# A new order of work for a decode block with its gradients: priorities, load gates and eviction bias

## The chip, the cores and the metric

The kernel runs on one core of a Trainium2 chip. Time is the device time in microseconds (us) of one execution, smaller is better. Times are given as the median of several runs; the profile is of one further execution, whose own time stands beside its span.

## The reference

The kernel computes one decode step of a transformer block, its output and the gradients of all inputs that have one. With `x` of shape 2 x 1 x 576 (two batch elements, one token each):

```python
xn = layernorm(x)
out = x + A(xn, k_cache, v_cache, wq, wo) + B(xn, w_gate, w_up, w_down)
# A: grouped-query attention, 32 query heads, 16 K/V heads, 4096 cached positions, head size 128
q = xn @ wq;  p = softmax(q @ k.T * 128 ** -0.5);  A = (p @ v) @ wo
# B: bilinear gated MLP, hidden width 4608
B = ((xn @ w_gate) * (xn @ w_up)) @ w_down
outputs = out, gradients of x, k_cache, v_cache, wq, wo, w_gate, w_up, w_down
```

All tensors are bf16. The K and V caches are 2 x 16 x 4096 x 128 (32 tiles of 1 MB each), and their gradients have the same size. The gradients are outer products of short vectors, so the kernel reads 92.48 MB, writes 92.48 MB, and does little arithmetic for each byte.

## The kernel before, in words

**Tiling.** The attention is cut into 16 steps (8 groups of two K/V heads, two batch elements); a step has two K tiles and two V tiles, each 128 x 4096 (1 MB). The MLP is cut into nine slices of 512 hidden columns, loaded in pairs. Sixteen SBUF buffers of 1 MB, called `big`, hold everything large: loaded K and V tiles, their transposed copies, gate and up weights, and the staging of results before they are stored. Six `ww` buffers hold wq, wo and w_down pieces.

**What a step does.** `turn` transposes a loaded tile on VectorE (DVE) in two halves (L418, 128x1024 f32). `score` multiplies it with the queries on TensorE (PE, L1205: 32 small matmuls per head). `softmax` and `dscore` are chains of small operations that hop between PE, DVE and ScalarE (ACT). `contract` (L1378) multiplies the probabilities with V, or the score gradients with K. `build_BD` makes a block-diagonal matrix on GpSimd (POOL, L1193). `head_outer` makes 1 MB of a cache gradient: PE writes outer products into one of three double PSUM banks `ps_o` (L1226), ACT or DVE casts them to bf16 in a `big` buffer (an eviction: L422 on ACT, L424 on DVE), and after four of these SP stores the buffer (`put`, L644). Gradients of the weights go the same way, by `rows_outer` (L675, 576 columns), `wide_outer` (L712) and `tails` (L756). In this layout out_2 is the gradient of K, out_3 that of V, out_4 of wq, out_5 of wo, out_6 and out_7 of gate and up, out_8 of w_down.

**Queues.** Every large load and store is issued by SP, one after the other (loads: L1087 for K and V, L1103 and L1107 for wq, L1112 for wo, L1126 and L1129 for gate and up, L1135 for w_down). An issue waits for the engines that fill or free its buffer, and for the landing of the transfer eight places before, since there are eight semaphores in turn. While SP waits, nothing behind it is issued. PE, ACT, DVE and POOL likewise run their instructions strictly in the program's order.

**What sets the order.** The kernel is written as some twenty generators (`turn`, `fronts`, `attend`, `dscores`, `load_kv` and so on) that yield their steps with an estimated cost: `PE(...)`, `DVE(0.34)`, `EV(1024)`, `DMA(...)`, `ACQ(...)` for a buffer. While the program is built, the class `Order` runs a small planner over them. It takes the step that can start first; of the steps that can start on the same engine no later than `SLACK[engine]` after it, it takes the one with the lowest priority number (`min` over the pair of priority and start), and the instructions are written down in that order. The priorities are the lists `PRI`: one number per step and kind of work, such as `out1` for the gradient of V. For POOL and SP the slack is 1e9, so there the priority alone decides among those that are known. `EV(cols)` is an eviction that may go to ACT or DVE: the planner takes the engine on which start, cost and bias are lowest, and DVE's bias is `cols / 1024 * BIAS`. `AT` holds load gates: a weight load may not be issued before the K or V load with that number (negative: no gate). Waits between engines are put in by the framework from the buffers that are read and written, so every order computes the same. On the chip nothing of the planner is left but the order.

Of the kernel before, what the change touches and what calls it, by code (L numbers as in the profile page):

```python
# [63 lines left out]
class Order:  # L64
# [88 lines left out]
    def run(self):  # L153
        while self.streams:
# [8 lines left out]
            if e is not None:  # L163
                t, _, s, e = min((c for c in cand if c[3] == e and c[0] <= t + SLACK[e]), key=lambda c: (c[1], c[0]))
            r = s.req
# [55 lines left out]
def EV(cols):  # L221
    return ("any", [("ACT", 0.16 + cols * 0.00083, 0.0), ("DVE", 0.145 + cols * 0.00104, cols / 1024 * BIAS)])

# [25 lines left out]
def DMA(engine, cost, nbytes, row=8192):  # L249
# [4 lines left out]
NBIG, NGU, NWW, NBD = 16, 1, 6, 3  # L254
CAP = {"kv": 7, "X": 15, "st": 4, "G": 2}
PRI = {
    "turn0": [7860.2, 2407.0, 17157.6, 2956.1, 16734.6, 2141.3, 12530.3, 5699.3, 6758.9, -15793.6, 4952.3,
        17816.5, -4355.6, 3251.1, -9409.0, 4354.9],
    "turn1": [-2637.0, 1283.6, 2414.9, -1225.0, -688.7, 9788.2, -4100.9, -1253.1, -13338.4, -4832.0, 7420.0,
        -4070.9, 3909.7, 3439.1, 24860.7, -8046.8],  # L260
    "W0": [5450.2, -3369.6, -7183.8, -9911.8, -15919.4, -4137.9, -34387.0, -4019.0, 12808.9, -13268.0, 2164.8,
        858.2, 9204.1, -21915.1, 27410.8, 5714.0],
    "W1": [-17967.7, -22162.9, -7000.7, 5860.0, -24123.9, -16750.0, -30695.7, -2322.8, 5885.0, -3621.0,
        -11899.3, -25222.7, 3484.3, 17013.0, 9916.4, -50953.1],
    "BD0": [25740.3, 53517.1, -7884.7, -22398.1, 2616.3, 11674.1, 17259.1, 25394.6, 12932.1, -24698.9, 82.6,
        -21163.1, -19953.8, 2102.0, 984.1, 27628.2],
    "BD1": [4904.3, 19218.9, 29867.0, 8059.0, 13597.2, -18879.4, 4713.9, 9772.5, 5835.6, -5651.5, 17495.2,
        -17656.1, 4419.6, -9395.9, -9786.8, -9239.0],
    "att": [-16176.1, -16637.1, -12810.8, -4457.5, 5838.0, -2018.2, -8215.2, -6231.2, -139.6, -20917.1,
        -13722.1, -15572.7, -14151.6, -16625.5, -17042.9, -18171.9],  # L270
    "dsc": [-9216.4, -7162.0, 2808.5, -17222.3, -6700.5, -8396.7, -1687.0, -19475.0, 11785.3, -22804.1,
        -13738.0, -25105.3, -15681.5, -29505.6, -519.1, -10067.7],
    "conv": [-73.6, -802.0, 808.6, 9911.0, -26988.3, -160.1, -15612.0, 2673.7, 20749.7, 20926.3, -10685.8,
        -20284.9, -8067.0, -18305.9, 1302.8, -5957.9],
    "con": [-3577.6, 11238.1, -10064.9, -5905.6, -14352.4, -9473.6, -2022.2, -31439.8, -4882.4, 8558.6, 647.3,
        -9042.3, -19399.9, -1065.6, -2476.7, 5001.6],
    "out0": [14046.8, 7812.4, 18755.6, 1578.1, 18723.0, 2045.3, -76.0, 4635.4, -4249.5, 66463.6, 1241.8,
        1393.3, 26893.0, 2322.7, -5773.2, 8123.2],
    "out1": [5636.0, 11913.1, 6780.7, 20338.1, 9883.3, -10850.1, 4408.6, 5776.7, 23687.8, 8619.3, 4031.8,
        17526.5, 33972.4, 22842.4, 6234.3, -887.1],  # L280
    "load": [3193.5, -640.3, 301.4, -16753.0, -8208.1, 1940.7, 9048.5, 16627.4, 5590.0, 7449.3, 8037.6,
        -5473.6, -4620.7, -10313.2, 936.0, -17873.6],
    "front": [11759.7, 4097.5, -19331.9, 3980.4, -367.3, 2898.4, -5242.4, -2790.9],
    "back": [-6458.1, -50.3, 4435.4, -11360.7, -12548.4, -12384.9, 955.9, -216.8],
    "mlp": [163.8, -787.4, -543.1, -7011.3, 1620.2, 3974.5, -1165.0, -2471.6, 1570.8],
    "mload": [-21609.9, -16477.7, -1378.7, -18105.2, 21631.6],
    "wload": [-1915.1, -8158.3, -15308.5, -12116.0, -16845.1, -3320.8, 11983.3, 9881.2, -10244.7, -12615.0,
        -8866.9, -18849.5, -7415.5, -20806.8, -24590.0, 27553.0],
    "wout": [-3012.7],
    "store": [2385.5],  # L290
    "fin": [-34927.4],
    "const": [23913.5],
}
AT = {
    "wq": [-17, 6, 5, 24, 30, -16, 50, -5],
    "wo": [-16, -13, -12, -7, 36, -20, -6, 52],
    "mlp": [2, 15, -12, 39, 82],
}
LATENCY, DRY, RATE = 0.5, 0.9, 1.009
LM, LAG, DRIFT = 0.67, 2.2, 0.009  # L300
CLK = 1.65
BIAS = 0.231829490117948
SLACK = {"PE": 0.0, "ACT": 0.11263292874939297, "DVE": 0.4671146883182233, "POOL": 1e9, "SP": 1e9}


def pr(name, i=0):
# [1227 lines left out]
```

## Time and profile before

| | |
|---|---|
| time, median of 3 runs | 474.47 us (472.94 to 476.24) |
| the profiled execution: its own time | 473.33 us |
| its span, first to last instruction | 471.3 us |
| mean granted TensorE clock | 0.718 of full |
| bytes moved by the DMA queue of SP | 184.96 MB, 395 GB/s over the span with the rest |
| instructions | 15,474 |

The page gives the busy time of each engine, and the span in 40 slices of 11.8 us: for each engine a digit for the tenths of the slice in which it was busy, for the DMA engines the share of time with packets, and the GB/s that they moved. An engine that waits in its own order for another shows idle time; the list of waits names whom it waited for. For SP, which only issues transfers, the list of waits says which engine's work the next transfer in its line was waiting for.

### The profile page before, as it was taken

To read this page: it belongs to the slowest core of one execution; us is meant where nothing else is said; L and a number is where in the kernel's file an instruction comes from. 1 tells how busy PE (TensorE), PEld (TensorE's weight loads), DVE (VectorE), ACT (ScalarE), POOL (GpSimd) and SP (SyncE) were. 2 spreads that over 40 slices of the span, in tenths; PEclk is the share of its full clock that TensorE was granted. 3 is DMA by queue.
4 is the path that set the end of the run, shared out by engine and by line. 5 is a ranking of instruction groups with operands and counts; after the bars stand their busy time and mean duration, and the time that the engine had idled before them with its cause. 6 is when DMAs were issued, how large, how long until landed. Compare 5 with 4: busy or idle time off the path is not lost. (4 is left out here: it accounts for less than half of the span.)

```text
span 471.3 us, 15474 instructions
## 1 busy us (share of the span) xinstructions
PE 368.2 (78%) x6636; PEld 214.5 (46%) x6636; DVE 372.2 (79%) x710; ACT 332.7 (71%) x502; POOL 147.2 (31%) x176
## 2 busy tenths in 40 slices
PE   0588688788787879795786779689699788988891
PEld 0455453454554344464353444464344544544461
DVE  9688787989857878878689748978867988888771
ACT  2158668678974967473798638877678788879881
POOL 3350242673330311300632354000744717034100
PEclk9987785879756677677866657956656677666785
DMA  8999999999999999999999999999999989999993
GB/s 309 407 407 415 392 388 378 357 417 411 423 420 419 396 419 422 428 411 417 414 418 386 385 418 421 414 397 360 412 412 377 424 302 424 423 406 396 425 406 127
DMA packets 40053, 185.96 MB, mean 395 GB/s; under 512 B 3496, under 2 KB 11184, under 8 KB 23600
## 3 DMA queue, kind: packets, MB, share of 16 engines
q1 hardware_dynamic: 39976, 184.96, 98.0%
q8 instruction: 52, 0.85, 0.7%
q14 instruction: 17, 0.14, 0.1%
q10 hardware_dynamic: 8, 0.00, 0.0%
HBM read 92.48 MB, written 92.48 MB: 392 GB/s over the span
## 5 line engine op out<-in xcount | busy, mean ns | idle before, releaser
L422 ACT CAST big<-ps_o 128x1024 bf16<-128x1024 f32 (+3 forms) x317 | 277.8, 951 | 41.2 <-PE ps_o L1226 20.4
L418 DVE STREAM_TRANSPOSE big<-big 128x1024 f32<-128x1024 f32 x146 | 176.1, 1223 | 9.0 <-DMA out_dram<-big 2.4
L1193 POOL TENSOR_TENSOR BD<-vr,mask 128x2048 bf16<-128x2048 bf16 x32 | 115.3, 3604 | 204.6 <-ACT vr L422 126.3
L424 DVE CAST big<-ps_o 128x1024 bf16<-128x1024 f32 (+3 forms) x73 | 80.3, 1100 | 20.3 <-PE ps_o L1226 7.5
L1205 PE MATMUL ps_m<-big,W 128*32 128x128 bf16 x2048 | 58.0, 275 | 7.7 <-issue 2.5
L1205 PEld LDWEIGHTS <-W 128*32 128x32 bf16 x2048 | 45.9, 121 | 26.4 <-issue 23.7
L1226 PE MATMUL ps_o<-BD,dd 32*128 32x512 bf16 x256 | 44.9, 460 | 13.9 <-ACT big L422 10.7
L1226 PE MATMUL ps_o<-BD,pp 32*128 32x512 bf16 x256 | 46.0, 490 | 11.1 <-ACT big L422 6.7
L1170 POOL COPY W<-rep 32x16 bf16<-32x16 bf16 x128 | 24.8, 194 | 49.3 <-DVE rep L951 40.2
L418 DVE STREAM_TRANSPOSE big<-ww 128x1152 f32<-128x1152 f32 (+1 forms) x25 | 33.0, 1318 | 1.2 <-PE ps_m L1378 0.7
L1378 PE MATMUL ps_m<-big,pp 128*32 128x512 bf16 x256 | 29.0, 543 | 2.3 <-DVE pp L418 1.5
L1378 PE MATMUL ps_m<-big,dd 128*32 128x512 bf16 x256 | 26.0, 496 | 1.3 <-DVE dd L418 0.8
L1226 PEld LDWEIGHTS <-dd 32*128 32x128 bf16 x256 | 11.6, 96 | 33.8 <-issue 27.9
L1226 PEld LDWEIGHTS <-pp 32*128 32x128 bf16 x256 | 10.6, 96 | 30.6 <-issue 26.6
L422 ACT CAST osb<-ps_m 128x512 bf16<-128x512 f32 x16 | 9.4, 587 | 20.1 <-PE ps_m L1378 20.0
L675 PE MATMUL ps_o<-dyr,hb 32*32 32x288 bf16 x288 | 17.7, 346 | 2.5 <-ACT big L422 1.9
L675 PE MATMUL ps_o<-dyr,R 32*32 32x288 bf16 x256 | 17.0, 389 | 1.8 <-ACT big L422 1.7
L422 ACT CAST sp<-ps_m 128x256 bf16<-128x256 f32 x24 | 9.1, 380 | 11.7 <-PE ps_m L1213 11.5
L712 PEld LDWEIGHTS <-xnr 32*128 32x128 bf16 x368 | 12.8, 120 | 9.0 <-issue 8.2
L1289 PE MATMUL ps_m<-small,G 128*128 128x1 f32 x32 | 8.6, 338 | 9.1 <-DVE D L849 3.1
L636 PEld LDWEIGHTS <-wm 128*32 128x32 bf16 x704 | 13.5, 116 | 4.4 <-issue 3.9
L967 PE MATMUL ps_m<-big,Wdy 128*128 128x128 bf16 x144 | 14.7, 282 | 0.9 <-DVE small L1330 0.6
(209 smaller groups left out, 479.9 us busy)
## 6 DMA issues: line engine op xcount, KB each, us to landing
out_dram<-big SPq DMA_DIRECT2D x74, 1024.0 KB, 14.2
big<-in_A_k_cache_dram SPq DMA_DIRECT2D x32, 1024.0 KB, 13.8
big<-in_A_v_cache_dram SPq DMA_DIRECT2D x32, 1024.0 KB, 13.4
out_dram<-big SPq DMA_DIRECT2D x17, 576.0 KB, 14.0
ww<-in_B_w_down_dram SPq DMA_DIRECT2D x9, 576.0 KB, 10.9
ww<-in_A_wo_dram SPq DMA_DIRECT2D x8, 576.0 KB, 11.2
ww<-in_A_wq_dram SPq DMA_DIRECT2D x8, 512.0 KB, 12.9
big<-in_B_w_gate_dram SPq DMA_DIRECT2D x4, 1024.0 KB, 14.2
```

The source lines that it names most:

```text
L418: nc.vector.transpose(out, in_)
L422: nc.scalar.copy(out, in_)
L424: nc.vector.tensor_copy(out=out, in_=in_)
L636: nc.tensor.matmul(dp[32 * q:32 * q + 32, :], lhsT=view(Wm[:], 0, P, 8 * pos(q, s), [[1, 32]]), rhs=view(X, 0, P, xoff(q, s), [[FS, blocks ...
L675: nc.tensor.matmul(o[32 * q:32 * q + 32, aa, 0:HD2], lhsT=view(t, 32 * q, 32, 2 * A + aa, [[4, 32]]), rhs=dyr[32 * q:32 * q + 32, k * HD2: ...
L712: nc.tensor.matmul(o[:, aa, j * P:(j + 1) * P], lhsT=xnr[32 * a:32 * a + 32, dc * P:(dc + 1) * P], rhs=rhs(a), start=True, stop=True)
L967: nc.tensor.matmul(dp, lhsT=Wdy[:, e, 2 * k:2 * k + P], rhs=view(X[:], 0, P, 64 * k + e, [[D, GH], [2, 32]]), start=(k == 0 and e == 0), s ...
L1170: nc.gpsimd.tensor_copy(view(W_t[t][w][:], 32 * a, 32, 6 + 8 * a, [[G * WW, 4], [WW, G], [1, 2]]), view(rep_t[grp[g]["qs"]][:], 32 * a, 32 ...
L1193: nc.gpsimd.tensor_tensor(BD_t[i][:], view(vr_t[v][:], 0, P, 0, [[0, 16], [1, Dh]]), view(mask16[:], 0, P, 0, [[1, 16], [0, Dh]]), ALU.mult)
L1205: nc.tensor.matmul(sc[32 * cq:32 * cq + 32, :], lhsT=view(W[:], 0, P, (be * G + l) * WW + 6 - 4 * c2 - 2 * l, [[1, 32]]), rhs=view(X[:], 0 ...
L1226: nc.tensor.matmul(o[:, k, :], lhsT=pr2[32 * c4:32 * c4 + 32, :], rhs=BD[32 * c4:32 * c4 + 32, 8 * l + 4 * h2:8 * l + 4 * h2 + 4, :], star ...
L1378: nc.tensor.matmul(ct[32 * j:32 * j + 32, :], lhsT=view(rT, 0, P, 4 * c + 2 * l, [[1, 32]]), rhs=kv_t[kvS[s][t][l]][:, Dh * c:Dh * (c + 4) ...
```

## The change

The change replaces numbers alone: all 22 lists of priorities, 15 of the 21 load gates, the eviction bias, and two of the slacks. No function is edited. The new numbers come from a search that judged each order by six replays with recorded courses of the granted clock and of the DMA landing lag.

```diff
 PRI = {
...
-    "out0": [14046.8, 7812.4, 18755.6, 1578.1, 18723.0, 2045.3, -76.0, 4635.4, -4249.5, 66463.6, 1241.8,
-        1393.3, 26893.0, 2322.7, -5773.2, 8123.2],
-    "out1": [5636.0, 11913.1, 6780.7, 20338.1, 9883.3, -10850.1, 4408.6, 5776.7, 23687.8, 8619.3, 4031.8,
-        17526.5, 33972.4, 22842.4, 6234.3, -887.1],
-    "load": [3193.5, -640.3, 301.4, -16753.0, -8208.1, 1940.7, 9048.5, 16627.4, 5590.0, 7449.3, 8037.6,
-        -5473.6, -4620.7, -10313.2, 936.0, -17873.6],
+    "out0": [22678.2, 12788.2, 42398.2, 31027.3, 49279.4, -11087.6, 5917.5, 42793.0, -20399.7, 57105.8,
+        29375.6, 687.4, 24906.2, -2550.4, -27276.1, 33869.5],
+    "out1": [19262.8, 2604.4, 2928.7, 23228.2, 21627.8, -10501.4, 15188.8, 7961.4, 18967.4, 20607.5, 11898.0,
+        33332.1, 33685.2, 22220.0, 30731.2, 4846.1],
+    "load": [27975.6, -31596.9, -27237.7, 3512.0, -22563.4, -17007.1, 4137.9, 25122.5, 5758.3, -9052.6,
+        -35105.2, 2003.7, -28928.7, 6812.9, 23298.4, -60102.7],
...
 }
 AT = {
-    "wq": [-17, 6, 5, 24, 30, -16, 50, -5],
-    "wo": [-16, -13, -12, -7, 36, -20, -6, 52],
-    "mlp": [2, 15, -12, 39, 82],
+    "wq": [-5, 7, 11, 24, 31, -18, 50, -5],
+    "wo": [-13, -2, -15, 2, 36, -14, 47, 53],
+    "mlp": [2, 16, -13, 39, 111],
 }
...
-BIAS = 0.231829490117948
-SLACK = {"PE": 0.0, "ACT": 0.11263292874939297, "DVE": 0.4671146883182233, "POOL": 1e9, "SP": 1e9}
+BIAS = 0.21111771427708687
+SLACK = {"PE": 0.0, "ACT": 0.11786185086953341, "DVE": 0.44815392421950667, "POOL": 1e9, "SP": 1e9}
```

`out0` and `out1` are the gradients of K and V, `load` the loads of K and V; the lists for the other kinds of work are replaced in the same way.

More of the change, by code (lines that the diff above doesn't have):

```diff
@@ L256 @@
 PRI = {
[L257 to L276, printed above, removed]
@@ L277 @@
-    "out0": [14046.8, 7812.4, 18755.6, 1578.1, 18723.0, 2045.3, -76.0, 4635.4, -4249.5, 66463.6, 1241.8,
-        1393.3, 26893.0, 2322.7, -5773.2, 8123.2],
-    "out1": [5636.0, 11913.1, 6780.7, 20338.1, 9883.3, -10850.1, 4408.6, 5776.7, 23687.8, 8619.3, 4031.8,
-        17526.5, 33972.4, 22842.4, 6234.3, -887.1],
-    "load": [3193.5, -640.3, 301.4, -16753.0, -8208.1, 1940.7, 9048.5, 16627.4, 5590.0, 7449.3, 8037.6,
-        -5473.6, -4620.7, -10313.2, 936.0, -17873.6],
-    "front": [11759.7, 4097.5, -19331.9, 3980.4, -367.3, 2898.4, -5242.4, -2790.9],
@@ L284 @@
[L284 to L292, printed above, removed]
+    "turn0": [12127.5, 6592.3, 21769.7, -2605.1, 16027.7, 11327.0, 15999.3, 39550.4, 10382.6, -7734.4, 35538.2,
+        24878.1, 2718.9, 31584.2, -26890.5, 2784.8],
@@ new lines @@
+    "turn1": [-17638.3, 2610.3, 11642.0, -23025.1, -666.2, 15183.7, -8429.9, 1153.7, -20487.3, 25941.4,
+        10117.7, 4947.3, -2272.2, 26485.5, 30929.5, -2450.0],
+    "W0": [17499.7, 23187.9, 23229.4, -24562.1, -25413.4, 21241.8, -52583.1, 25355.3, -4026.7, -26992.9,
+        -2792.0, -39509.0, -20712.1, -23397.7, -38581.5, -1973.1],
+    "W1": [-68220.0, -3785.6, -5692.6, -26672.7, -32830.2, -16110.0, -12761.0, -19860.2, 22087.6, 15126.8,
+        -21980.3, 8805.5, -32643.6, 50340.4, -9766.7, -46949.6],
@@ new lines @@
+    "BD0": [33847.1, 15885.5, -3782.4, -11229.3, 24201.3, 31507.4, 16705.2, 36715.7, 22613.4, -26234.1,
+        -2581.7, 109848.8, -44765.9, -8040.0, -3442.2, 23039.7],
+    "BD1": [6023.1, 63457.9, 25871.9, 3200.3, 32198.5, -18814.1, 12365.4, 26532.9, 45847.1, -51895.6, 27362.3,
+        -76393.3, 2863.2, -15443.1, -42340.1, -14044.7],
+    "att": [-30329.0, -12134.6, -9680.1, 2262.2, -4349.2, 5413.2, -20317.8, -14023.7, -15815.4, -22206.1,
+        -49797.4, -334.9, -19593.2, -20211.8, -68161.8, -27358.0],
@@ new lines @@
+    "dsc": [-23906.4, -34630.7, -2728.5, -23998.0, -19328.5, -8575.3, -10061.5, -15550.8, 13655.4, -23902.2,
+        -28324.1, -40880.7, -28538.6, -56867.0, -5830.5, -12006.5],
+    "conv": [-12341.8, -11809.0, -28772.8, 4652.6, -75297.7, -7012.1, -20664.5, 17461.5, 27449.8, 21658.4,
+        -6850.8, -13921.3, -10206.6, -13431.8, 19855.6, -8570.5],
+    "con": [-42900.2, 17788.3, 198.2, -17106.1, -21976.4, -3999.9, 7207.3, -22623.4, -6927.6, 21516.2, 20924.0,
+        -13390.2, -118243.2, -7700.5, 19019.7, 14780.5],
@@ new lines @@
+    "front": [22268.9, 9016.8, -3195.4, -925.0, -11488.9, -5594.5, -10266.7, 2816.4],
+    "back": [8334.8, 3131.5, 10704.4, -20159.0, -16008.9, -4698.0, -5371.8, 1371.3],
+    "mlp": [-5535.1, -15193.4, -221.7, -14784.7, -3773.2, 8812.5, 807.2, 180.8, 6936.3],
+    "mload": [-52363.2, -31069.0, 25120.7, -76464.9, 11215.5],
+    "wload": [26545.8, -25483.3, -28807.4, 17849.2, -51701.7, -14210.9, -857.7, -9350.9, -12979.9, -24368.0,
+        -173571.7, -10429.5, -11015.2, 13337.1, -10805.0, 6634.5],
@@ L293 @@
+    "wout": [-3917.3],
+    "store": [6257.1],
+    "fin": [-45349.8],
+    "const": [46567.9],
 }
 AT = {
-    "wq": [-17, 6, 5, 24, 30, -16, 50, -5],
-    "wo": [-16, -13, -12, -7, 36, -20, -6, 52],
-    "mlp": [2, 15, -12, 39, 82],
+    "wq": [-5, 7, 11, 24, 31, -18, 50, -5],
+    "wo": [-13, -2, -15, 2, 36, -14, 47, 53],
+    "mlp": [2, 16, -13, 39, 111],
 }
```

## The prediction

> **What bounds the kernel now.** First the page: span, engines, slices.
>
> ```profile
> span 471.3 us, 15474 instructions
> PE 368.2 (78%) x6636; PEld 214.5 (46%) x6636; DVE 372.2 (79%) x710; ACT 332.7 (71%) x502; POOL 147.2 (31%) x176
> PEclk9987785879756677677866657956656677666785
> DMA  8999999999999999999999999999999989999993
> GB/s 309 407 407 415 392 388 378 357 417 411 423 420 419 396 419 422 428 411 417 414 418 386 385 418 421 414 397 360 412 412 377 424 302 424 423 406 396 425 406 127
> ```
>
> DMA packets are nearly always in flight, but the bytes are not even: 420 to 428 GB/s in good slices, 302 to 397 in ten others. The table of stretches gives these as times (columns: length, busy time of PE, weight loads, DVE, ACT, POOL, clock, DMA share, GB/s).
>
> ```profile
> 47.00:94.00 47.00, 36.48 (x711) 21.69 (x710) 38.48 (x71) 33.40 (x54) 18.96 (x26) 0.75 0.98 379
> 94.00:247.00 153.00, 123.89 (x2403) 74.53 (x2402) 122.50 (x218) 110.88 (x167) 43.30 (x47) 0.72 1.02 417
> 247.00:271.00 24.00, 17.00 (x234) 9.22 (x233) 19.33 (x28) 17.90 (x27) 7.04 (x18) 0.63 0.98 386
> 306.00:389.00 83.00, 71.33 (x1235) 39.98 (x1224) 67.83 (x120) 62.20 (x94) 30.25 (x32) 0.62 0.99 384
> 400.00:459.00 59.00, 53.55 (x928) 29.48 (x916) 48.36 (x91) 49.84 (x73) 12.20 (x4) 0.71 1.02 412
> ```
>
> Against the 417 of 94 to 247, the stretch 47 to 94 loses 4.3 us (38/417 x 47), 247 to 271 loses 1.8, 306 to 389 loses 6.6: 12.7 us that a better order could win. Why the queue thins is in SP's own order of time:
>
> ```profile
> 60.62 0.34 SPq L1087 DMA_DIRECT2D big<-in_A_k_cache_dram  x1
> 67.11 0.34 SPq L644 DMA_DIRECT2D out_dram<-big  x1
> 67.55 1.63 SPq L1087 DMA_DIRECT2D big<-in_A_k_cache_dram  x1
> 73.71 9.61 SPq L644 DMA_DIRECT2D out_dram<-big  x4
> 83.41 0.38 SPq L1087 DMA_DIRECT2D big<-in_A_v_cache_dram  x1
> ```
>
> SP is one line: from 60.96 to 67.11 it holds a store whose evictions are not done, and nothing behind it is issued. Bytes issued less bytes whose packets ended: 0.13 MB are left at 67.4, 0.16 at 81.3, 0.48 at 253.7, 0.50 at 315.5, 0.24 at 379.6, against 3 to 5 MB in the good stretches. So in the thin places the engines set the time, in 94 to 247 the bytes do. Among the engines, the waits:
>
> ```profile
> SPq L644 <- DVE big L424: 83.6, 35, 9.1
> SPq L644 <- ACT big L422: 82.8, 59, 5.2
> ACT big L422 <- PE ps_o L1226: 20.4, 23, 2.7
> PE ps_o L1226 <- ACT big L422: 17.4, 42, 0.9
> ```
>
> PE and ACT hold each other through three PSUM tiles; neither is idle long. The page's chain that ended last, some 70 us of tail, says the same: engines, hardly an issue or a DMA.
>
> ```profile
> PE 7%; ACT 4%; DVE 2%; issue 1%; ACTq 0%; DVEq 0%
> ```
>
> **The change, part by part.** The amount of work is the same: 13,011 weight loads and matmuls, 220 transfers of 184.9 MB, no new operation. Laid side by side, the built programs differ in 78 of SP's 220 places: 17 to 32, 42 to 48, 55 to 67, 80 to 106, 112 to 123, 160 to 171, 201 to 208, and the last three. From 124 to 200 SP differs in nine places only. For each transfer I add up what must have ended on each engine before it (mean durations of the groups; for matmuls a group's busy time by its count) and the MB issued before it, in both programs.
>
> *Evictions.* Three of 128x576 leave DVE for ACT, and some small ones cross either way: ACT +2.1 us (3 x 0.656, the rest from the rows of 0.17 to 0.38), DVE -2.1 (3 x 0.748 and the like). ACT idles 139 us, DVE 99, so value 0; -2.1 if DVE alone bound, +2.1 if ACT did.
>
> *Places 17 to 32.* The eighth V load passes wq and wo of group 1; qt, wq and wo of group 2 slip from 22, 23, 30 to 30, 31, 32. The V load waits for PE until 29.2; with 1.11 MB of weights now behind it the queue has 2.46 - 1.11 = 1.35 MB then: no hole. The weights are wanted at 51.9 and 83.7 (first matmuls of L934 for these groups), more than 15 us after they would land. At 34 the programs agree again: 26.1 MB, DVE 61.2 us, PE 45.4, ACT 38.0 in both. The first thin place stays: 0.
>
> *Places 33 to 48.* Store 37 needs 3.0 us less PE (ready 71.1 for 73.7 by before's clock times), 39 needs ACT +1.0 (81.9 for 81.0), 40 PE -0.9 and DVE -1.7 (82.7 for 83.0). MB ahead are equal. Store 40 ends the hole: -0.3, bounds -1.7 and +0.9. The K load moved ahead of the gate weights goes into a queue that refills anyway: 0.
>
> *Places 55 to 106.* Here bytes bind (417), so what is first matters only if an engine then stalls. A transpose now writes a tile whose store (54) lands about 2.4 us after DVE gets there; the longest stall of before here, ACT at 151.2 for 4.2 us, falls by 0.8. Between them 0, bounds -0.8 and +2.4.
>
> *Places 112 to 123.* V-gradient stores now go ahead of K-gradient stores. Readiness: 248.4, 251.0, then 262.5 for the last, where before had 249.2, 253.3, 253.9, 257.6; the delivered bytes reach that place at 260.2. The 262.5 is read off ACT's old course, which idles there for PE; by work alone the last store needs ACT +1.1, DVE +0.6, PE -0.5. Load 124 behind it needs DVE +3.5 (19.3 of 24.0 us busy, so room for it). I take +1.0, nearest to the work row; bounds -2.0 (the gain of the second) and +4.9.
>
> *Places 160 to 171.* A row store that was ready at 329.7 and sat until 338.6, behind weights that SP could not issue because the transfer eight before each had to land, goes ahead of two of them: its buffer is free earlier, the MB in eight places are the same. The last of the three stores after it needs ACT +1.6: +0.3, bounds 0 and +1.6.
>
> *Places 201 to 220.* Same sum; ACT's work ahead goes from +1.6 to +2.5, so +0.9 in the tail, where ACT is the largest entry in the chain that ended last (3% of the span). DVE -2.6. I take +0.3; bounds -0.5 and +0.9.
>
> Sum: -0.3 + 1.0 + 0.3 + 0.3 = +1.3. The profiled execution took 473.33 (span 471.3 and 2.0 around), so 474.6 by it; from the median 474.47 it is 475.8. I say **475.0**, between the two and 0.4 over the first, and put the rivals 0.4 over their sums likewise. About 1% is what a measurement of this kernel tells from no change.
>
> The clock: the granted clock of this trace is only ever 0.5 or 1.0, in stretches of multiples of 3.41 us, 268 of 449 us at 0.5; a group of 32 L1205 matmuls takes 0.66 us at 1.0 and 1.04 at 0.5. A stretch more at 0.5 costs 3.41 x (1 - 0.66/1.04) = 1.25 us of PE. The Trainium skill, "TensorE: Matmul & The Clock Gate", section on the clock gate, says that the clock is halved after an idle window of about 3.4 us and full after a busy one. The two values and the step agree; the cause does not, for after 12 us no PE gap is over 3.05 us and yet the clock is halved 60% of the time. By its rule an order that widens that 3.05 us gap would pay one more half window, 1.25 us by the rows.
>
> **The rivals.**
>
> *No stall left in 94 to 247 (faster).* For it: ACT and DVE wait 7.4 us for stores to land there (5.3 and 2.1), and most of the moved transfers stand there. Against: the bytes bind. If the stretch ran at its best slice, 428, it would win (1 - 417/428) x 153 = 3.9, and with the 247 to 271 hole closed (1.8) 5.7: 468.0. Chance 0.17.
>
> *ACT's line at the four stores (slower).* If ACT really reaches the last of places 120 to 123 at 262.5, every transfer behind moves by 4.9, since the order behind is unchanged and nothing catches up, and ACT's +0.9 in the tail is added: 5.8, so 479.5. For it: PE waits 17.4 us for ACT already. Against: ACT is idle 25% of 247 to 271. It decides from 260.2 us on, when the queue is empty. Chance 0.20.
>
> *The clock falls another way.* Ten stretches of 3.41 us more or fewer at 0.5, of 79, are 12.5 us of PE, and about half of it carries to the end, as PE is 7 of 14 per cent in the chain that ended last: 468.8 or 481.2. Three runs of one order spread over 3.3 us, so this is rarely more. Chance 0.06, even sides.
>
> *The order acts as before.* It does not do nothing, since 78 places differ, but the thin places keep their MB: this is the forecast, chance 0.57, own range 470 to 479.
>
> **How the numbers follow.** Likeliest 475.0. The bounds of the parts add up to -5.0 and +10.7; all upper ones together are unlikely, so the range goes from 467.0 (the first rival with two clock stretches won, 2.5 of PE at half) to 481.0 (ten lost; the second rival lies inside). Faster by over 1%: the first rival 0.17 and 0.03 of the clock, 0.20. Slower: 0.20 and 0.03, 0.23. The rest 0.57.
>
> **What would show it.** Right: thin queues again near 67, 81, 315 and 379 us; GB/s of 94 to 247 within 413 to 422; the four stores issued over some 9 us before load 124, at 257 to 261; ACT busy 2 us more, DVE 2 us less. Wrong: a hole of over 3 us at the four stores; a thin place gone; a mean clock off 0.718 by over 0.03.

## The result, and the profile after

The kernel after takes 471.87 us (median of 20 runs, 470.59 to 474.17), the kernel before in the same series 473.88 (20 runs, 472.03 to 476.24). The ratio is 0.9961, with a 95% interval from 0.9947 to 0.9974: 1.8 us faster (1.2 to 2.5). That is inside the 1% that the prediction called no change, and inside its range, but on the other side of zero from its 475.0. The profiled execution took 471.37 us, with a span of 469.6.

The page of after: span, busy times, and of the 40 slices the granted clock, DMA share and GB/s.

```profile
span 469.6 us, 15459 instructions
PE 370.8 (79%) x6636; PEld 217.5 (46%) x6636; DVE 369.5 (79%) x705; ACT 334.3 (71%) x507; POOL 146.8 (31%) x176
PEclk9978897767757668776675767956656658566977
DMA  8999999999999999999999999999999989999995
GB/s 317 404 413 403 363 390 419 409 416 421 418 416 420 399 421 406 412 415 419 399 418 404 386 418 424 408 413 342 413 416 393 424 270 416 423 413 413 424 368 176
```

ACT has 1.6 us more work than before, DVE 2.7 less. The span is 1.7 shorter although PE is busy 2.6 longer, with a mean granted clock of 0.710 for 0.718. The same five stretches as before (length, busy time of PE, weight loads, DVE, ACT, POOL, clock, DMA share, GB/s):

```profile
47.00:94.00 47.00, 36.81 (x748) 21.89 (x736) 40.60 (x76) 35.68 (x58) 20.14 (x30) 0.79 1.01 395
94.00:247.00 153.00, 124.59 (x2383) 77.20 (x2375) 119.53 (x211) 108.87 (x169) 43.14 (x50) 0.68 1.02 414
247.00:271.00 24.00, 15.86 (x219) 8.90 (x216) 19.43 (x31) 17.30 (x27) 5.82 (x13) 0.68 1.00 394
306.00:389.00 83.00, 71.53 (x1153) 38.22 (x1144) 64.67 (x115) 62.35 (x93) 30.04 (x32) 0.60 0.98 382
400.00:459.00 59.00, 53.09 (x915) 28.44 (x907) 48.32 (x87) 50.10 (x74) 13.61 (x4) 0.69 0.98 401
```

The first stretch moves 395 GB/s where before had 379, and 247 to 271 has 394 for 386; the last has 401 for 412. SP's own order of time shows what happened to the first thin places (a place is a number in SP's line of 220 transfers):

```profile
65.77 0.34 SPq L644 DMA_DIRECT2D out_dram<-big  x1
66.21 0.38 SPq L1087 DMA_DIRECT2D big<-in_A_k_cache_dram  x1
66.69 0.79 SPq L1087 DMA_DIRECT2D big<-in_A_v_cache_dram  x1
68.97 11.35 SPq L644 DMA_DIRECT2D out_dram<-big  x4
80.42 0.55 SPq L1087 DMA_DIRECT2D big<-in_A_v_cache_dram  x1
```

The store at 65.8 now has 1.26 MB of earlier transfers still moving (0.13 in before), the stores of places 39 and 40 have 0.99 and 1.19 MB (0.16 and 0.08), and the issue of place 41 ends at 81.0 us instead of 83.8. Two of the four thin places that the forecast expected to stay are gone, a sign that the prediction had named as one against it. It looks as if this were the gain. The experiments say that it is not.

SP waits more for ACT than before (112.3 us in total for 82.8) and a little more for DVE (90.6 for 83.6); PE and ACT wait for each other a little less. These totals do not tell the gain either.

### The profile page after: what moved, and what is told of

It is laid out like the page before. It is cut to its first block, busy times and chain, and to the rows that moved or that the text cites. A ratio compares the mean times of both kernels' runs of the same rounds, so it can differ in the third digit from the quotient of the medians.

```text
span 469.6 us, 15459 instructions
## 1 busy us (share of the span) xinstructions
PE 370.8 (79%) x6636; PEld 217.5 (46%) x6636; DVE 369.5 (79%) x705; ACT 334.3 (71%) x507; POOL 146.8 (31%) x176
## 4 chain that ended last, share of the span: by engine, by line
PE 42%; ACT 18%; DVE 18%; DMA 12%; issue 5%; POOL 2%; SPq 2%; ACTq 0%; DVEq 0%; POOLq 0%
ACT big L422 15%; DMA out_dram<-big 10%; DVE big L418 8%; PE ps_m L1378 8%; PE ps_o L1226 7%; PE ps_m L1205 7%; PE ps_o L675 4%; PE ps_m L841 3%; DVE big L424 3%; DMA big<-in_A_v_cache_dram 3%; PE ps_m L967 2%; PE ps_m L636 2%; POOL BD L1193 2%; PE ps_o L712 1%; SPq L1129 1%
## 5 line engine op out<-in xcount | busy, mean ns | idle before, releaser
L422 ACT CAST big<-ps_o 128x1024 bf16<-128x1024 f32 (+4 forms) x319 | 279.7, 950 | 40.3 <-PE ps_o L1226 18.2
L424 DVE CAST big<-ps_o 128x1024 bf16<-128x1024 f32 (+2 forms) x71 | 78.2, 1102 | 15.8 <-PE ps_o L675 5.2
L1205 PE MATMUL ps_m<-big,W 128*32 128x128 bf16 x2048 | 57.1, 274 | 5.5 <-ACT osb L422 0.7
L1226 PE MATMUL ps_o<-BD,dd 32*128 32x512 bf16 x256 | 48.8, 489 | 12.7 <-ACT big L422 9.2
L1205 PEld LDWEIGHTS <-W 128*32 128x32 bf16 x2048 | 45.4, 121 | 21.9 <-issue 18.6
L1226 PE MATMUL ps_o<-BD,pp 32*128 32x512 bf16 x256 | 42.1, 461 | 10.4 <-ACT big L422 6.7
L1378 PE MATMUL ps_m<-big,dd 128*32 128x512 bf16 x256 | 27.5, 518 | 1.5 <-DVE dd L418 0.6
L422 ACT CAST osb<-ps_m 128x512 bf16<-128x512 f32 x15 | 8.9, 590 | 15.9 <-PE ps_m L1378 12.6
L675 PE MATMUL ps_o<-dyr,hb 32*32 32x288 bf16 x288 | 16.5, 346 | 1.1 <-ACT big L422 0.9
L967 PE MATMUL ps_m<-big,Wdy 128*128 128x128 bf16 x144 | 14.9, 285 | 3.1 <-DVE small L1283 2.0
L636 PEld LDWEIGHTS <-wm 128*32 128x32 bf16 x704 | 13.4, 115 | 6.3 <-issue 5.1
L841 PE MATMUL ps_m<-big,Wdy 128*128 128x128 bf16 x162 | 15.6, 272 | 0.6 <-DVE small L1291 0.4
## 6 DMA issues: line engine op xcount, KB each, us to landing
big<-in_A_k_cache_dram SPq DMA_DIRECT2D x32, 1024.0 KB, 12.4
```

The source lines that it names most:

```text
L422: nc.scalar.copy(out, in_)
L424: nc.vector.tensor_copy(out=out, in_=in_)
L636: nc.tensor.matmul(dp[32 * q:32 * q + 32, :], lhsT=view(Wm[:], 0, P, 8 * pos(q, s), [[1, 32]]), rhs=view(X, 0, P, xoff(q, s), [[FS, blocks ...
L675: nc.tensor.matmul(o[32 * q:32 * q + 32, aa, 0:HD2], lhsT=view(t, 32 * q, 32, 2 * A + aa, [[4, 32]]), rhs=dyr[32 * q:32 * q + 32, k * HD2: ...
L841: nc.tensor.matmul(dh, lhsT=Wdy[:, e, 2 * k:2 * k + P], rhs=view(X[:], 0, P, 64 * k + e, [[D, FC], [2, 32]]), start=(k == 0 and e == 0), s ...
L967: nc.tensor.matmul(dp, lhsT=Wdy[:, e, 2 * k:2 * k + P], rhs=view(X[:], 0, P, 64 * k + e, [[D, GH], [2, 32]]), start=(k == 0 and e == 0), s ...
```

## The experiments

**How an order is cut in two.** At places 34, 50, 71, 134, 174 and 209 of SP's line both planners have issued the same transfers and written down the same steps of every engine; only the order inside the pieces differs. So the pieces can be exchanged. The 4,216 steps of both orders were recorded (which generator goes on, and on which engine an eviction runs), and the experiments replace the planner's choice by such a list. The work stays the same:

```diff
         while self.streams:
-            cand = [...]                       # all steps that can start
-            t, _, s, e = min(...)              # by SLACK and PRI
+            # a written list of steps: the first of it that can start
+            s, e = next(...)
```

The whole list of before is the kernel before, instruction for instruction, and that of after the kernel after. Below, `before[a:b]` stands for the steps of places a to b in before's order. Differences in us are the ratio's, against runs of before on the same chip.

The parts: **head** (places 1 to 50), **middle** (51 to 134), **late** (135 to 209), **tail** (210 to 220).

### One part alone

```diff
-steps = before[1:220]
+steps = after[1:50]   + before[51:220]                   # e1_head
+steps = before[1:50]  + after[51:134]  + before[135:220] # e2_middle
+steps = before[1:134] + after[135:209] + before[210:220] # e3_late
+steps = before[1:209] + after[210:220]                   # e4_tail
```

> The written order of the kernel after for SP's places 1 to 50 and for all engine work planned up to there, the order before from place 51 on. Theory A (head and tail): the lead that the trace of after shows at place 71 (1.6 us) and at place 134 (1.1 us) comes from here and lives to the end: 1.0 to 1.5 us less than before, places 34 and 41 at about 66.1 and 81.0 us as after has them (67.5 and 83.8 before). Theory B (the tail alone): the lead of the head is eaten by the buffers that come free no earlier in 94 to 247, so within 0.5 us of before. Theory C (the prediction as it stands): 0.3 us less, and the thin places at 67 and 81 us stay.

Measured: 472.79 us, ratio 0.9977 (0.9960 to 0.9995), -1.1 us.

> The order before, with the order of after for places 51 to 134. Theory A: after gives back about 0.3 us between places 50 and 134 (its lead goes from 1.4 at place 84 to 1.1 at place 134), so within 0.5 us of before. Theory B: 0. Theory C: 1.0 us more than before, from the four stores at places 120 to 123, of which the load at 124 is later than 259.2 us.

Measured: 476.04 us, 1.0038 (1.0019 to 1.0056), +1.8 us.

> The order before, with the order of after for places 135 to 209. Theory A: after loses 0.7 to 1.6 us here (lead 1.1 us at place 134, 1.0 at 174, 0.7 at 182, and 0.6 late at 209), so up to 1 us more than before if that lateness reaches the end, 0 if the tail hides it. Theory B: 0. Theory C: 0.6 us more, 0.3 at places 160 to 171 and 0.3 at 201 to 208.

Measured: 473.37 us, 0.9989 (0.9977 to 1.0002), -0.5 us.

> The order before up to place 209 and the order of after from there on: the 2 KB store of out_1 goes behind the two 64 KB tail stores, and seven evictions and two products of the last 20 us change places. Theory A: the two tail stores no longer wait behind it, and the last store leaves 1.2 to 1.8 us earlier: 1.0 to 1.8 us less than before. Theory B: the whole gain, 2.0 us less. Theory C: 0, since the prediction gave the last three places no price.

Measured: 473.66 us, 1.0000 (0.9983 to 1.0017), 0.0 us.

The tail is nothing, although the two traces differ by 2.3 us there (place 209 to the end of the span: 25.7 in before, 23.4 in after). Over the profiles of all twenty kernels of this study that stretch lies anywhere between 23.3 and 26.2, whichever tail they have. The four parts add up to +0.2, and all together give -1.8, which suggests that parts help each other.

### One part left out

```diff
-steps = after[1:220]
+steps = before[1:50]  + after[51:220]                    # e5_not_head
+steps = after[1:50]   + before[51:134]  + after[135:220] # e6_not_middle
+steps = after[1:134]  + before[135:209] + after[210:220] # e7_not_late
+steps = after[1:209]  + before[210:220]                  # e8_not_tail
```

> The order after, with the order of before for SP's places 1 to 50. The four parts alone gave, against before, head -1.1, middle +1.8 (profile +3), late -0.5, tail 0, which adds up to +0.2 us, while all four together give -1.9: two parts that help each other must account for 2.1 us. Additive theory: middle, late and tail give +1.3 us. If head and middle are the pair: +1.3 too, since the middle stands behind the wrong head. If middle and late are the pair: -0.8. If the sum is only noise: about 0.

Measured: 475.06 us, 1.0020 (0.9995 to 1.0045), +0.9 us against before.

> The order after, with the order of before for places 51 to 134. Additive theory: head, late and tail give -1.6 us against before, and if the middle is a loss by itself (+1.8) this should be the quickest of all. If the middle pays only together with another part, this stands at -1.6 too while after stands at -1.9, so that the middle costs nothing in its place; if it pays by itself in the place behind the new head, this is slower than after by more.

Measured: 472.61 us, 0.9974 (0.9953 to 0.9995), -1.2 us.

> The order after, with the order of before for places 135 to 209. Additive theory: head, middle and tail give +0.7 us against before. Head and middle as the pair: -1.4. Middle and late as the pair: +0.7.

Measured: 473.96 us, 1.0002 (0.9981 to 1.0023), +0.1 us.

> The order after up to place 209 and that of before from there on. The tail alone gave 0. If it is worth nothing behind any order: -1.9 us against before, like after. If the tail's order (the small store of out_1 behind the two 64 KB stores) pays only where the stores before it come as in after, where the last three places gained 2.5 us in the trace: -0.4 to -0.9 us.

Measured: 471.58 us, 0.9962 (0.9944 to 0.9981), -1.8 us.

The tail is again nothing. Without the head, or without the late part, the gain is gone. The middle is dear only where the head is that of before, and the trace says why. DVE's transposes in e5 and in after, from the timeline (start, length; in brackets the idle time ahead and what ended it):

```profile
95.45 2.37 DVE L418 STREAM_TRANSPOSE big<-big 128x1024 f32<-128x1024 f32 x2
103.23 1.25 DVE L418 STREAM_TRANSPOSE big<-big 128x1024 f32<-128x1024 f32 x1 [5.34 <-DMA big<-in_A_k_cache_dram]
104.57 1.22 DVE L418 STREAM_TRANSPOSE big<-big 128x1024 f32<-128x1024 f32 x1
```

```profile
95.13 1.23 DVE L418 STREAM_TRANSPOSE big<-big 128x1024 f32<-128x1024 f32 x1
96.45 1.22 DVE L418 STREAM_TRANSPOSE big<-big 128x1024 f32<-128x1024 f32 x1
104.05 1.38 DVE L418 STREAM_TRANSPOSE big<-ww 128x1152 f32<-128x1152 f32 x1 [3.28 <-DMA out_dram<-big]
```

The order of after puts both transposes of one K tile (steps `turn` of the K tile that before loads at place 48) directly behind their predecessors; in before they stand some 7 us further back (two rows of before's timeline):

```profile
104.13 1.20 DVE L418 STREAM_TRANSPOSE big<-big 128x1024 f32<-128x1024 f32 x1
105.88 1.20 DVE L418 STREAM_TRANSPOSE big<-big 128x1024 f32<-128x1024 f32 x1
```

The order of after also issues that K load at place 42, ahead of six weight loads, where its issue ends at 82.1 us. With the early transposes and the late load (issued at about 91 behind 3.2 MB, landed at 103.1) DVE waits 4.7 to 5.7 us, and PE behind it stands idle for 4.4 to 5.1. The prediction had given this move of the load a value of 0.

### The head in pieces

The head differs in three things: SP's places 17 to 32 (weights of group 2 later, the eighth V load earlier), SP's places 42 to 48 (that K load), and the engines' order between about 58 and 80 us, where a few products of the stores come earlier, with their evictions. The engines do the same in places 1 to 34 of both.

```diff
-steps = after[1:220]
+steps = before[1:34] + after[35:220]                      # e9_not_first
+steps = after[1:34]  + before[35:50] + after[51:220]      # e10_not_second
+head = SP of after, other engines of before               # e11_head_sp
+head = SP of before, other engines of after               # e12_head_eng
```

> The order after, with the order of before for SP's places 1 to 34 alone (the V load behind the weights of group 1, the weights of group 2 at places 24, 25 and 30; no other engine's order differs there). The whole head is worth 2.9 us in this company (after -1.9 against before, without the head +1.0). Theory D, deferred weights: 1 MB less of weights ahead of the K and V loads brings the loads of the next units, and so the stores at places 34 to 41, forward; without it about +1.0 us against before. Theory E, engines: the four products and evictions of the second slab of stores that after puts ahead of a contraction (PE, ACT and DVE between about 58 and 80 us) close the holes at 67 and 81 us; this kernel keeps them and stays at -1.9.

Measured: 472.52 us, 0.9982 (0.9964 to 1.0000), -0.9 us.

> The order after, with the order of before for places 35 to 50 (SP's weights 42 to 48 ahead of the K load, and the engines' order of before between about 58 and 80 us). Theory D: the deferred weights stay, so -1.9 us against before. Theory E: about +1.0. If the K load ahead of six weights at 42 is the cause: about +1.0 too, told apart by the next two.

Measured: 474.32 us, 1.0017 (0.9999 to 1.0036), +0.8 us.

> The order after, but up to place 50 all engines other than SP keep the order of before; SP's order is that of after. Theory D: -1.9 us against before, Theory E: about +1.0, and the thin places at 67 and 81 us are back.

Measured: 472.13 us, 0.9973 (0.9954 to 0.9991), -1.3 us.

> The order after, but up to place 50 SP keeps the order of before; the engines' order is that of after. Theory D: about +1.0 us against before. Theory E: -1.9, and the thin places at 67 and 81 us stay away.

Measured: 475.05 us, 1.0035 (1.0015 to 1.0055), +1.7 us.

Neither theory holds as written. The K load at place 42 decides: the two kernels that have it (e9, e11) keep about half the gain or more, the two that lack it (e10, e12) have none of it left, at +0.8 (-0.1 to +1.7) and +1.7 (+0.7 to +2.6), and their traces have the wait at 98 to 104 us again (DVE 4.99 and 5.67). And e11 shows what the holes at 67 and 81 us are worth. SP's order of time in e11:

```profile
67.50 0.34 SPq L644 DMA_DIRECT2D out_dram<-big  x1
74.10 9.27 SPq L644 DMA_DIRECT2D out_dram<-big  x4
83.46 0.38 SPq L1087 DMA_DIRECT2D big<-in_A_v_cache_dram  x1
```

These are before's times within 0.4 us, with 0.65, 0.47 and 0.25 MB outstanding at places 34, 39 and 40, and the issue of place 41 ending at 83.8 us; yet the time is that of after within the intervals. The 2.8 us that the trace of after gains at place 41 come from the engines' order there, and these runs find no gain from them at the end.

### The K load alone, the pair, and the rest of the middle

```diff
-steps = before[1:220]
+steps = before, K load of place 48 at 42                  # e13_k_load
+the same, with after[135:209]                             # e14_k_load_late
+steps = before[1:71] + after[72:134] + before[135:220]    # e15_second_half
+K load at 42, with after[51:134]                          # e16_pair
```

> The order before with one move: SP issues the K load of place 48 at place 42, ahead of the six weight loads; every engine's order stays. Pair theory: the load pays only where VectorE's two transposes of that K come early (in before they come at 104 and 106 us, when it has long landed, in after at 97 to 100 us), so within 0.5 us of before. Load theory: the early load by itself lifts the rest, -1.1 us, all that the head gave when it stood alone.

Measured: 473.88 us, 1.0002 (0.9986 to 1.0018), +0.1 us.

> The move of the K load and the order of after for places 135 to 209, the rest as before. Load theory: -1.1 and -0.5 to -0.9, so -1.6 to -2.0 us against before, as good as after with a fifth of its edits. Pair theory: -0.5 to -0.9, what the late places give alone.

Measured: 472.61 us, 0.9974 (0.9956 to 0.9993), -1.2 us.

> The order before, with that of after for places 72 to 134 alone. Places 51 to 134 cost 1.8 us, and the trace shows VectorE waiting 4.7 us for the K load at 98 to 103 us there. If that wait is the whole cost, this kernel, which leaves it out, is within 0.5 us of before. The prediction's term for the four stores at places 120 to 123 is +1.0 us: then this is +1.0.

Measured: 473.53 us, 0.9999 (0.9978 to 1.0019), 0.0 us.

> The move of the K load and the order of after for places 51 to 134. Pair theory: VectorE no longer waits at 98 us, the middle's +1.8 goes, and the two together give -0.5 to -1.5 us. Load theory: -1.1 from the load, +1.8 less the wait of some 2 us, so -0.5 to -1.1 too; if the middle costs 1.2 us even behind the early load, as the kernels with and without it suggest where the late places are those of before, about 0.

Measured: 473.47 us, 0.9992 (0.9977 to 1.0008), -0.4 us.

The pair theory holds: the early load is worth nothing by itself and saves some 2 us where the transposes are early; together the two parts are worth little (-0.4, -1.1 to +0.4). The programs of e2 and e16 differ in that one load's place alone, and in their difference from before by 2.2 us. The middle's loss is that wait: without places 51 to 71 it is 0. So the four stores at places 120 to 123, in their new order, show no cost (0.0, -1.0 to +0.9).

### The late part in two

```diff
-steps = before[1:220]
+steps = before[1:134] + after[135:174] + before[175:220]  # e17_late1
+steps = before[1:174] + after[175:209] + before[210:220]  # e18_late2
```

> The order before, with that of after for places 135 to 174: a weight load goes three places later, two stores earlier, and twelve evictions change sides. The late places as a whole give -0.5 us alone, -1.2 with the early K load, -2.0 where all else is as after. First theory, this half carries it (after leads by up to 3.7 us at places 162 to 165 in the traces): -0.5 to -0.9 us. Second theory, the other half carries it: 0. Third theory, the prediction's terms: +0.3.

Measured: 472.24 us, 0.9965 (0.9943 to 0.9987), -1.7 us.

> The order before, with that of after for places 175 to 209: two stores go three places later, seventeen evictions change sides, and products and contractions of the last two units change places. First theory: 0. Second theory: -0.5 to -0.9 us. Third theory, the prediction's terms: +0.3.

Measured: 473.75 us, 0.9996 (0.9974 to 1.0017), -0.2 us.

The first half, 40 places of which SP's order differs in 160 to 171 alone, does by itself about what the whole change does. That is likely too much: e3, which has both halves, gave -0.5. One difference stands out in POOL's line in before, and in e17 (the timeline; it builds the block-diagonal matrices, 3.6 us each):

```profile
330.93 7.17 POOL L1193 TENSOR_TENSOR BD<-vr,mask 128x2048 bf16<-128x2048 bf16 x2 [38.66 <-ACT vr L422]
339.47 3.60 POOL L1193 TENSOR_TENSOR BD<-vr,mask 128x2048 bf16<-128x2048 bf16 x1 [1.37 <-DVE vr L424]
346.89 3.60 POOL L1193 TENSOR_TENSOR BD<-vr,mask 128x2048 bf16<-128x2048 bf16 x1 [3.82 <-PE ps_o L1226]
```

```profile
330.53 7.17 POOL L1193 TENSOR_TENSOR BD<-vr,mask 128x2048 bf16<-128x2048 bf16 x2 [39.02 <-ACT vr L422]
339.13 3.60 POOL L1193 TENSOR_TENSOR BD<-vr,mask 128x2048 bf16<-128x2048 bf16 x1 [1.43 <-DVE vr L424]
344.06 3.60 POOL L1193 TENSOR_TENSOR BD<-vr,mask 128x2048 bf16<-128x2048 bf16 x1 [1.33 <-DVE vr L424]
```

The matrices live in three buffers, and PE makes eight pairs of products from each. In before PE does six pairs of the first matrix, all eight of the second, and only then the last two of the first, so that the fourth matrix goes into the buffer of the second, and POOL waits 3.8 us until PE has read that one for the last time, at 346.9. In the order of after PE does all eight pairs of the first matrix and then those of the second; the first buffer is free from about 340, and POOL waits only for the vector that DVE, where before had ACT, casts at 343.7. The fourth matrix starts 13.4 to 14.0 us after the first in all eleven kernels that have after's places 135 to 174, and 15.9 to 16.1 in all nine that have before's: no overlap. From place 146 to 174 the eleven take 58.0 us on the average and the nine 59.9 (difference 1.9, standard error 0.3; single profiles scatter by more).

It looks as if POOL's wait were the cause. The traces speak against it. These are three rows of PE and POOL in before, the rows between them left out, and then one of PE in e17:

```profile
311.03 0.30 PE L1205 MATMUL ps_m<-big,W 128*32 128x128 bf16 x3 [0.79 <-issue]
352.49 1.85 POOL L1170 COPY W<-rep 32x16 bf16<-32x16 bf16 x8 [2.00 <-DVE rep L951]
354.27 0.61 PE L1226 MATMUL ps_o<-BD,dd 32*128 32x512 bf16 x2
```

```profile
309.09 1.04 PE L1205 MATMUL ps_m<-big,W 128*32 128x128 bf16 x32
```

In before the fourth matrix is finished at 350.5 us, and PE first reads it at 354.3, 3.8 us later; in all twenty kernels it is ready at least 2.6 us before PE reads it. POOL then stands idle for 2.0 us more, until DVE has done its part. So nothing is seen to wait for the matrix that comes late. And much of the lead is older than the wait. From place 146 to POOL's first matrix the eleven are already 1.0 us quicker (standard error 0.3), from there to place 172 they gain 0.0 (0.3), and the other 0.9 (0.2) come between places 172 and 174. Ahead of the first matrix an idle time separates the two groups: in all nine PE stands still for 0.6 to 1.1 us inside a group of 32 matmuls of L1205 near 311 us, waiting for nothing that the profile shows ("issue"); none of the eleven has this, although PE's order there is the same. Before that, between 288 and 301 us, a few products and evictions stand in another order, and no run takes these apart from the rest. So the runs show what this piece is worth; why is open.

### All together

If each piece has one price, and the middle's price is due only where the K load is late, the nineteen measured ratios (the eighteen and after itself) can be fitted, each weighted by its interval. Three prices are enough: places 1 to 34, -0.66 us (standard error 0.20); the wait for the K load, +2.16 (0.26), where transposes are early and the load late; places 135 to 174, -0.89 (0.17). The misfit is 12.3 for 16 degrees of freedom, no more than chance gives, so no help beyond the pair is needed. With all pieces free the others come out at -0.19 (0.25) for the K load by itself, -0.01 (0.28) for the engines' order in the head, -0.10 (0.25) for places 72 to 134, +0.29 (0.38) for 175 to 209, +0.30 (0.25) for the tail. After should then be -1.5; it is -1.8. The wait shows in the traces as well: from place 50 to 84 the four kernels with it take 72.4 to 73.3 us, the other sixteen 70.1 to 72.0, 2.0 us less on the average. None of the eighteen has a lower ratio than after.

## Why the prediction was wrong

**Places 160 to 171, forecast +0.3: the step that failed most.** Alone, the piece that holds them gave -1.7 us (-2.7 to -0.6), and -0.9 (standard error 0.17) over all comparisons: the term has the wrong sign. The sum counted work ahead of each *store*, ACT +1.6 before the last of three, and only at places where SP's line differs; the rest of the piece it took as equal. In the traces 1.0 of the 1.9 us are won before place 160 is issued, at places where SP's line is the same in both and only the engines' order had changed. What wins them stays open. The wait of 3.8 us of POOL for PE, which the prediction did not look at either, is gone in the order of after, but no work is seen to wait for its result.

**Places 112 to 123, forecast +1.0.** Measured 0.0 (-1.0 to +0.9) with the rest of before around it, and from place 84 to 134 the kernels take 107.9 us on the average with either order (107.3 to 108.7 over all twenty). The +1.0 was taken from ACT's extra work ahead of the last store (+1.1); that work did not show in the time, and the runs do not tell why. The slower rival, ACT reaching the last of them at 262.5, did not come: the issue of place 124 ended at 257.9.

**Places 17 to 32, forecast 0.** The fit gives -0.7 for them. They were never run alone, and no place of the traces shows where it comes from (place 16 to 34 takes 47.6 us with, 47.9 without, standard error of the difference 0.5). Whether the deferred weights are what helps, and how, stays open. These three terms, +0.3 that was -0.9, +1.0 that was 0.0 and 0 that was -0.7, make up 2.9 of the 3.1 us between the forecast sum of +1.3 and the measured -1.8.

**Places 33 to 48, forecast -0.3.** The piece that was reckoned, stores 37 to 40, moved by more than was forecast (place 41: -2.8 us) and brought nothing (-0.01, standard error 0.28). The K load, given 0, is worth 0 by itself; but the working did not see that the transposes of that tile were put forward too, so that without the load's move 2 us would have been lost. Both halves were in the change, and the net of 0 came out right by luck.

**Places 55 to 106, forecast 0 with bounds of -0.8 and +2.4.** The net is right: e16, which has all of these places and the early K load, stands at -0.4 (-1.1 to +0.4). The two stalls behind it did not come as reckoned. DVE waits at most 0.7 us for the store of place 54 in the kernels with this order and no late K load, where 2.4 was forecast; the 3.28 us in the rows of after above is for another store, and e9, e11 and e16 do not have it. ACT's stall near 151 us, which was to fall by 0.8, is 4.2 in after as in before.

**Places 201 to 220, forecast +0.3**, is not contradicted by 175 to 209 and tail (+0.29 and +0.30, each about one standard error from 0). The small store of out_1 behind the two tail stores, left without a price, shows no price (e4 and e8). Evictions: the busy times moved about as forecast (ACT +1.6 for +2.1, DVE -2.7 for -2.1), their price was not measured apart.

**What bounds the kernel.** The prediction read it off the thin queue: 12.7 us to be won where the GB/s are low. For the first stretch that reading failed. Closing the holes at 67 and 81 us did not change the time, and e17, with the holes of before (0.08, 0.03 and 0.03 MB at places 34, 39 and 40, and 378 GB/s in 47 to 94), is as fast as after. Its line of that stretch and SP's order in it:

```profile
47.00:94.00 47.00, 36.22 (x709) 21.44 (x708) 38.34 (x72) 33.26 (x55) 18.92 (x26) 0.75 0.97 378
```

```profile
67.32 0.34 SPq L644 DMA_DIRECT2D out_dram<-big  x1
73.92 9.60 SPq L644 DMA_DIRECT2D out_dram<-big  x4
```

A hole there is the sign that the engines are behind; that filling it by doing the stores' products sooner only puts other work of the same engines later is an argument, which no run shows. The holes near 315 and 379 us stayed in after, so what they are worth was not tested. Of the rivals, the faster one (no stall left in 94 to 247) did not occur: 414 GB/s for 417.

**The clock.** The four kernels with the wait for the K load have a PE gap of 4.4 to 5.1 us, and the granted clock after it, from 104 to 112 us, is 0.50 in all four. The Trainium skill, "TensorE: Matmul & The Clock Gate", Part 1, says that an idle window of about 3.4 us halves the clock. The trace does not tell whether it was that: six kernels with the same middle and no gap over 2.6 us there have 0.50 to 0.60 as well.

## What to carry to other kernels

A thin transfer queue shows where engines are late, not that the queue is worth filling: ask whether the engine that fills it gains time, or only does something else later. When a new order is judged, follow every early consumer to its load; here one load moved past six others was what kept a 2 us loss away. When a wait disappears, look at when its result is next read before calling it the gain: here a matrix was ready 3.8 us before its reader came, and the lead was in part older than the wait. Price the engines' order also where the transfer line is unchanged. Parts of an order can be cut out at places where both orders have done the same work, and a part that looks bad alone may be one half of a pair.

## What was not expected of the hardware

A single pair of traces misleads at the level of 1 to 3 us. Kernels with the same order up to a place pass it up to 3.5 us apart: e3 and before have the same order up to place 134, and e3 issued place 124 of it 3.5 us later and place 128 0.6 us earlier. The stretch from place 209 to the end took 23.3 to 26.2 us for nearly the same work. What did repeat to some tenths in twenty profiles were distances between two steps of one chain, such as the 15.9 to 16.1 us between POOL's two matrices. The time of a load was set mostly by what stood ahead of it in the queue: the late K load, issued behind some 3.2 MB, landed 12.4 us later (90.70 to 103.14 in e5); its own 1.05 MB and those 3.2 at the 417 GB/s of that part are 10.1 us, which leaves 2.3.
